# One core, eight batches: the filter loaded in four parts, and a new hand-kept order of the work

## The chip, the cores and the metric

The kernel runs on 1 core of one Trainium2 chip, as one launch. The time is device microseconds (us) of that core, the median over runs. The kernel before was run three times: 953.13, 957.69 and 958.69 us, median 957.69 us.

## What is computed

For each of 8 batches with S = 3136 rows, D = 256 features and 64 features of z:

```python
scores = z @ z.T / S                     # 3136 x 3136, symmetric
attn   = maximum(scores, 0) ** 2
x      = u * (attn @ v)
proj   = x @ w_proj                      # 256 -> 768, cut into x1, x2, x3
conv   = irfft(rfft(x2, axis=1) * rfft(filter_fft, axis=0), n=S)
out    = (x1 * conv * x3) @ w_out
```

All inputs and the output are float32; the kernel multiplies in bf16 and sums in float32. The filter is one matrix of 3136 x 256, the same for all batches, and its spectrum H is worked out once, beside batch 0.

## The kernel before

**Tiles.** The 3136 queries of a batch are cut into seven chunks (`CHUNKS`, 512 wide but for the last two, 256 and 320). For each chunk TensorE (PE) makes scores, two key tiles of 128 at a time, into one of three PSUM pairs `ps_s` (`score_mm`, L1632). ACT or DVE takes the positive part into `R_t` (L1790, L1792), ACT or DVE squares it into `A_t` (L1799, L1801). PE then multiplies `A_t` by v into the accumulator `ps_o_t` (`weigh`, through the helper at L462). Since the scores are symmetric, a chunk's squares are also the squares of later chunks, turned. SP sends them through a transposing DMA (`mirror`, L1739) into the mirror tiles M1 (for the next chunk) and M2e or M2o (for the one after), which the trace calls `M_t`, `M2e_t` and `M2o_t`; `weigh` reads them in place of new scores. M1, M2e and M2o have one buffer each, `A_t` has nine. An `A_t` buffer is free when its weighing is done and its transposes have landed.

**From chunk to output.** When a chunk is weighed, DVE multiplies it by u (`xe`, L1843) into `xT_t`. PE projects it to the gates and to x2 (`add_proj`); x2 goes through the first stage of the Fourier transform (`dft1`, matrix T1), and SP puts the result to DRAM (L950). When all seven chunks of a batch are there, `add_spectrum` loads the columns (L979; L994 in the last batch), runs the second stage forward, multiplies by H, runs it back, and puts the result (L1300). `add_end` loads that by chunk (L1014), runs the last stage (matrix T4), multiplies by the gates (L1351), multiplies by `w_out` and stores (L1383). Batch b's spectrum and end run beside batch b+1's attention; only the last batch has nothing beside it but work held back for it: the ends of three chunks of batch 6 (kind Z) and the gates of batch 7 (kind G).

**What sets the order.** A planner in the kernel's Python (`Plan`) gives out the work. The string `ORDER` says, letter by letter, what kind of work PE does next (S scores, W and v the two halves of a weighing, A, B, Q, Z, G and their second halves a). The string `ENGINES` says for each eviction whether ACT or DVE does it. SP, POOL, ACT and DVE take what is ready first by the planner's own reckoning of durations and DMA landings (`LATE_...`, `moves`, `late`). So the instruction streams of all engines are fixed when the kernel is built; on the chip each engine goes through its stream in order and waits where data is missing. What the planner takes for a landing changes only the order.

**POOL's casts.** Float32 input comes in as bf16 through casting DMAs that POOL issues: v (`load_rows`, L561), u (`cast_u`, L542), z (`cast_rows`, L542), the filter (`load_filter`, L635). They are issued in bundles: when the u product of a chunk is made, POOL copies one element of it (`await_x`, L551, "the tick" below) and then issues that chunk's bundle. In batch 0 the ticks of chunks 0, 1 and 2 also carry a part of the filter each (`filt_cuts`), and the third part carries `w_out` with it. The bundle that a chunk's tick carries for the next batch's v is set by `cuts`.

**The last batch's end.** `FINAL` is the order in which the chunks of batch 7 are ended: 0, 2, 4, 6, 1, 3, 5.

**Fillers.** Where the planner sees PE idle, it puts in matmuls of the identity (L662), whose results nobody reads.

Of the kernel before, what the change touches and what calls it, by code (L numbers as in the profile page):

```python
# [24 lines left out]
LATE_PUT, LATE_LOAD, LATE_TURN, LATE_M, LATE_C, LATE_D2 = 1.2, 1.2, 1.3, 0.3, 0.8, 1.0  # L25
# [9 lines left out]
FINAL = (0, 2, 4, 6, 1, 3, 5)  # L35
# [7 lines left out]
    "ASSASSSWWvSAWAWSvSvSvWSWWSvSWvSvWSvWWSvSWvWSvvSSSWSvWWWWWAWavSvAWWSWBvWSvSavWvWSSvvvvvBBaAaaWSWWAWSavWWWAAav"  # L43
    "aSWWSWSvvAvavSWSvAWWavSvSvvvBSSWABWavSWWWBSSvavvvBSWWWWaWSWSvvWvvSvASWaSvBvaSWvSWAWWWWWaBWaSvWvWWSvAvvSSavWv"
    "BvaSWvASaSAAaavvSSAaWWWWWWSSvvvWWAASvvaWvWaAvvvQSaWWWSWWWAAavWavWvQWSQvvWSSvWWSvAWavvSvvSvAaSSSWWWSvWvAWvSvW"
    "aSWWWSSvAvavAvWSSWWaWQSvQvvSvQASaWWWSWSSvWAWaWvSvWWSvSSvWSvAvWAWaSvWavSvvvQQAaWSWSvWSAWaWQSvWQWWWSQvSvvvWWQv"
    "QWWvSQvvvvASAaaWWQQvWvSWWSQvWvSWSvWQQvvWvSWQWQWWSvvQvSvAAaaWWQWWSQvAvavSWWSvSvWSvSAvaSWWWWASvSWavSWSvSAvavAB"
    "aaAWWavvWASWaASWaAvvWaBWvaWBWSavvSvSWSBvBaaAWavSBWaWWASvaWASWvWvSWavSWWWSBWSavvWASvavvvvABSaaWWAWaASvaSWAvaA"
    "WAaaWSvWSvWSvvSAvSaWSWWBSvvWaBWvSavvSSBaSWWWWSWSSvWvvvWSSWBvWWWSSvaWWSBvvaAvaSvSvvAQAaWaWWSWSAWWSavWQvSvvvvS"
    "SSWWWWSWWQvSvAvvvvAaSaWWWQWQvvWQSSWvvWWWQQvWvWSSvSvWWvSQvQvvAAaSaWWWQQWWWSQvSvvSWQWvvWAWavSAvWWWvSvSavvSvAAa"  # L50
    "AaWaSWWWWWAWSavSvWQvSvWvvSWQSvvvSAAaSWavWWAWaSvvWWSSSWvWWASvvvSaWWWvWSSvvvAvBSaaWWSWSWWWBSvavSvWSvSWAvaAvSWa"
    "BWSvaAvaAWWaWSBvavAvvaAAaSaWSWWSvBAaaSWvWSSvWSWWASvaWvAvavBSWWavSBvaWWvSSvvABaaWBWWSaSvvWSWBSaWAvaSvvQQvWWWS"
    "WQAvaSvWvABaWaWQvSvQvAASaaWWWSSvWWSvAvaAvQWWQvSWWQvvWvQBaWaWSvWBSvaSvvAAaSaWWQSSvWWSvQQvvWQWWSWQvSvWvAWWSvaA"
    "vSvaQWWSvQvAASaaWWWWSvvSWvSBvWWWSavSvvSWABvSaWaAvaAAaWSavWWSSvWWSWvSSvWBvaWWWSWAWAaWvavvSASavvvvSABaaWWSSvvW"
# [294 lines left out]
def kernel(  # L349
# [16 lines left out]
    NT = (N2 + 1) // 2  # L366
# [259 lines left out]

    def load_filter(t0, t1):
        x = rows_n1(moe_filter_fft)
        n = min(8, NT - 1 - t0)
        for j in range(2):  # L630
            a = NT + t0 if j else NT - t0 - n
            src = x[:, a : a + n]
# [495 lines left out]


    gates = {}  # L1130
    inverses, stores_late, last_load = [], [], []

    def add_proj(b, c, xt, x_):
        cw, nt = CHUNKS[c], len(tiles[c])
# [782 lines left out]
```

## Time and profile before

| What | Value |
|---|---|
| runs | 953.13, 957.69, 958.69 us |
| the profiled execution's own time | 959.67 us |
| its span, first to last instruction | 957.9 us |
| PE busy | 920.8 us, 11974 matmuls |
| DVE, ACT, POOL busy | 836.7, 825.9, 202.6 us |
| bytes moved by DMA | 168.40 MB, of these 37.30 MB by POOL's queue |

The profiled execution is 1.98 us over the median of the three runs, and 1.8 us of its time lie outside the span. The views used below are: the page (busy times, and the span in 40 slices); the windows (busy time of each engine in a stretch, with the granted clock of PE and the mean busy share of the 16 DMA engines); the waits (who waited for whom); the chain that ended last, in order of time; the timeline of one engine (start, duration, what; in brackets the idle time before it and what ended that); and the DMA view of a stretch. SPq and POOL rows that say DMA are the issue of a DMA, not its transfer.

### The profile page before, as it was taken

The numbers are of one execution on the slowest core, as the hardware profiler recorded it, in microseconds if no ns is written. First come the engines' busy times: TensorE is split into PE (matmuls) and PEld (weight loads), VectorE is DVE, ScalarE is ACT, GpSimd is POOL, SyncE is SP. The second block draws the span as 40 slices with busy tenths as digits, with TensorE's granted clock in tenths as the row PEclk, the third lists the DMA queues.
The fourth block names the chain that finished last, engine by engine and source line by source line (L and its number), as shares of the span: only waits on it lengthen the run. The fifth ranks groups of instructions, "written<-read, shape, count | busy, mean of one in ns | idle before, by whom it ended". The sixth has DMA issues, their size and how long they took to land.

```text
span 957.9 us, 28971 instructions
## 1 busy us (share of the span) xinstructions
PE 920.8 (96%) x11974; PEld 543.9 (57%) x11974; DVE 836.7 (87%) x1182; ACT 825.9 (86%) x927; POOL 202.6 (21%) x438
## 2 busy tenths in 40 slices
PE   7995999999999999999999999999999999999986
PEld 3442654557655675557655576546755566556644
DVE  8994699997999999999999779999889888899684
ACT  6783689999899898898989989999899999999672
POOL 5231211212122121222021120212212221001130
PEclk8997999999999999999999999999999999999997
DMA  9899778999999599998899997999899968887767
GB/s 156 144 173 119 158 131 147 178 199 170 183 190 182 116 187 180 210 200 167 162 190 201 202 207 171 186 169 187 185 165 183 185 123 174 181 205 146 208 187 225
DMA packets 321701, 168.40 MB, mean 176 GB/s; under 512 B 231990, under 2 KB 297334, under 8 KB 321568
## 3 DMA queue, kind: packets, MB, share of 16 engines
q1 hardware_dynamic: 290656, 127.54, 65.2%
q0 software_dynamic: 29872, 37.30, 26.3%
q8 instruction: 94, 1.54, 0.7%
q10 hardware_dynamic: 1040, 1.70, 0.6%
q14 instruction: 39, 0.32, 0.1%
HBM read 90.26 MB, written 53.35 MB: 150 GB/s over the span
## 4 chain that ended last, share of the span: by engine, by line
PE 82%; DMA 6%; DVE 5%; ACT 2%; issue 2%; SPq 2%; ACTq 0%; DVEq 0%; POOL 0%; POOLq 0%
PE ps_o_t L462 49%; PE ps_s L462 20%; PE ps_s L1632 10%; PE ps_s L1033 3%; DMA M2e_t<-A_t 2%; DMA spec<-gs_t 1%; DVE R_t L1792 1%; DVE xT_t L1843 1%; DMA zT_t<-zn_t 1%; DMA A_t<-spec 1%; SPq L1439 1%; DVE A_t L1801 1%; ACT R_t L1790 1%; DMA M_t<-A_t 0%; DMA spec<-uT_t 0%
## 5 line engine op out<-in xcount | busy, mean ns | idle before, releaser
L462 PE MATMUL ps_o_t<-A_t,v_t 64*128 64x512 bf16 (+4 forms) x4736 | 506.4, 355 | 0.6 <-DVE xT_t L1843 0.4
L462 PEld LDWEIGHTS <-v_t 64*128 64x128 bf16 (+1 forms) x6510 | 295.2, 98 | 217.7 <-issue 20.0
L1790 ACT ACTIVATE R_t<-ps_s 128x1024 f32<-128x1024 f32 (+4 forms) x353 | 331.8, 962 | 41.5 <-PE ps_s L1632 34.9
L1799 ACT ACTIVATE A_t<-R_t 128x1024 bf16<-128x1024 f32 (+3 forms) x283 | 275.8, 994 | 28.1 <-DMA M2e_t<-A_t 11.4
L1801 DVE TENSOR_TENSOR A_t<-R_t 128x1024 bf16<-128x1024 f32 (+4 forms) x209 | 229.6, 1116 | 15.1 <-ACT R_t L1790 12.6
L1632 PE MATMUL ps_s<-zT_t 64*128 64x512 bf16 (+5 forms) x1209 | 191.2, 355 | 14.0 <-ACT R_t L1790 10.4
L1792 DVE TENSOR_SCALAR R_t<-ps_s 128x1024 f32<-128x1024 f32 (+4 forms) x159 | 175.5, 1113 | 33.0 <-PE ps_s L1632 27.9
L551 POOL COPY tick<-xT_t 1x1 bf16<-1x1 bf16 x54 | 9.5, 177 | 640.2 <-DVE xT_t L1843 640.2
L462 PE MATMUL ps_s<-xT_t,wp 64*128 64x512 bf16 (+2 forms) x848 | 118.7, 351 | 0.4 <-ACT R_t L1790 0.4
L1632 PEld LDWEIGHTS <-zT_t 64*128 64x128 bf16 (+1 forms) x1209 | 67.6, 97 | 51.2 <-issue 6.3
L502 ACT ACTIVATE x_t<-ps_s 128x1024 bf16<-128x1024 f32 (+3 forms) x82 | 76.5, 941 | 19.9 <-PE ps_s L462 18.7
L462 PE MATMUL ps_o_t<-M_t,v_t 64*128 64x512 bf16 (+4 forms) x864 | 93.3, 352 | 0.0
L1843 DVE SCALAR_TENSOR_TENSOR xT_t<-ps_o_t,uT_t 128x256 bf16<-128x256 f32 (+2 forms) x224 | 71.3, 380 | 11.3 <-PE ps_o_t L462 5.6
L1256 DVE TENSOR_TENSOR xh<-xh,H 128x2048 bf16<-128x2048 bf16 x60 | 72.3, 1217 | 1.8 <-ACT xh L502 1.6
L1165 DVE TENSOR_TENSOR gate_t<-ps_s,x_t 128x512 bf16<-128x512 f32 (+2 forms) x104 | 59.7, 615 | 14.6 <-PE ps_s L462 10.4
L1351 DVE TENSOR_TENSOR yT_t<-ps_s,gate_t 128x1024 bf16<-128x1024 f32 (+2 forms) x51 | 55.1, 1084 | 14.0 <-PE ps_s L462 12.0
L462 PE MATMUL ps_s<-wp,xT_t 64*128 64x256 bf16 x800 | 65.3, 269 | 0.4 <-DVE s_t L506 0.2
L462 PEld LDWEIGHTS <-wp 64*128 64x128 bf16 x896 | 47.3, 94 | 30.2 <-issue 3.2
L542 POOL DMA_DIRECT2D un_t<-in_u_dram x112 | 59.9, 554 | 9.5 <-issue 6.8
L561 POOL DMA_DIRECT2D v_t<-in_v_dram x112 | 58.7, 542 | 8.7 <-issue 7.0
L462 PE MATMUL ps_s<-wo,yT_t 64*128 64x256 bf16 x732 | 58.6, 270 | 0.7 <-DVE yT_t L1351 0.4
L462 PE MATMUL ps_o_t<-M2e_t,v_t 64*128 64x512 bf16 (+2 forms) x440 | 52.0, 353 | 1.5 <-DVE xT_t L1843 1.4
(174 smaller groups left out, 887.4 us busy)
## 6 DMA issues: line engine op xcount, KB each, us to landing
out_dram<-ost_t SPq DMA_DIRECT2D x56, 256.0 KB
spec_in_t<-spec SPq DMA_DIRECT2D x56, 192.0 KB
spec<-gs_t SPq DMA_DIRECT2D x56, 192.0 KB
v_t<-in_v_dram POOLq DMA_DIRECT2D x80, 128.0 KB, 5.0
un_t<-in_u_dram POOLq DMA_DIRECT2D x80, 128.0 KB, 5.7
spec<-s_t SPq DMA_DIRECT2D x40, 256.0 KB
conv_in_t<-spec SPq DMA_DIRECT2D x34, 256.0 KB
out_dram<-ost_t POOLq DMA_DIRECT2D x12, 256.0 KB, 3.7
```

The source lines that it names most:

```text
L462: last = matmul(o[ds(i, n)], w[:, ds(i, n)], m, **kw)
L502: nc.scalar.activation(out_, in_, AF.Copy)
L542: nc.gpsimd.dma_start(out=t[ds(j * N1, N1), lo - t0 : hi - t0, :], in_=x[:, n2 : n2 + hi - lo, :])
L561: nc.gpsimd.dma_start(out=t[ds(j * N1, N1), ds(v_at(a), (b - a) * D)], in_=r[:, n2 + a - lo : n2 + b - lo, :].rearrange("p t d -> p (t d)"),)
L1165: nc.vector.tensor_tensor(g[:, :, ::-1] if h == 0 else g, p, x, ALU.mult)
L1256: nc.vector.tensor_tensor(x, x[:, 1].unsqueeze(1).to_broadcast([P, 2, 2, 2 * D]), h, ALU.mult)
L1632: matmul(o[ds(m, n)], zt[h, ds(t * P + m, n)], q, start=True, stop=True)
L1790: nc.scalar.activation(r, p, AF.Relu)
L1792: nc.vector.tensor_single_scalar(r, p, 0.0, ALU.max)
L1799: nc.scalar.activation(a, r, AF.Square)
L1801: nc.vector.tensor_tensor(a, r, r, ALU.mult)
L1843: nc.vector.scalar_tensor_tensor(x[:, ::-1] if h == 0 else x, f, inv_s2, ut, ALU.mult, ALU.mult)
```

## The change

The diff does five things. The filter comes in four parts where it came in three: the old third part, rows 16 to 24 and `w_out`, becomes one of rows 16 to 20 on the tick of chunk 2, and one of rows 20 to 24 with `w_out` on the tick of chunk 3. Batch 1's v comes one or more chunks later. `FINAL` becomes 5, 6, 0, 2, 4, 1, 3, and the last batch's gates stand in their queue in that order. Four of the planner's guesses of landings are raised. `ORDER` and `ENGINES` are other strings of the same letters. The products stay the same; fewer of the matmuls of scores and weighings are cut into two of 64 columns (the planner does that where they stand beside work of kind Q), and there are 9 fillers where there were 16.

```diff
-LATE_PUT, LATE_LOAD, LATE_TURN, LATE_M, LATE_C, LATE_D2 = 1.2, 1.2, 1.3, 0.3, 0.8, 1.0
+LATE_PUT, LATE_LOAD, LATE_TURN, LATE_M, LATE_C, LATE_D2 = 2.2, 1.2, 1.3, 0.3, 0.8, 2.5
...
-FINAL = (0, 2, 4, 6, 1, 3, 5)
+FINAL = (5, 6, 0, 2, 4, 1, 3)
...
-    "ASSASSSWWvSAWAWSvSvSvWSWWSvSWvSvWSvWWSvSWvWSvvSSSWSvWWWWWAWavSvAWWSWBvWSvSavWvWSSvvvvvBBaAaaWSWWAWSavWWWAAav"
...
+    "ASSASWSSAWSvSASSWSWSvvWWWWSvSWBvWSvSvSWSvvvSWWvvSAWSvaASWWSWWavSvvWWSvSWWWSvWvWvWvSvvvSAaBSWWavWWSvBSvWWWWaW"
...
     def load_filter(t0, t1):
         x = rows_n1(moe_filter_fft)
-        n = min(8, NT - 1 - t0)
+        n = min(t1, NT - 1) - t0
...
-    filt_cuts = ((0, 8), (8, 16), (16, NT))
-    filt_ld = [Task(lambda e, x=x: load_filter(*x), {"POOL": 1.6}, moves=3.3, late=4.0) for x in filt_cuts]
+    filt_cuts = ((0, 8), (8, 16), (16, 20), (20, NT))
+    filt_ld = [Task(lambda e, x=x: load_filter(*x), {"POOL": 1.6}, moves=0.42 * (x[1] - x[0]), late=4.0) for x in filt_cuts]
...
-        return on("SP", go, 0.55, deps, [home.slots], moves=0.235 * nt, late=1.0 if home is cut_in else -1.0), box
+        return on("SP", go, 0.55, deps, [home.slots], moves=0.235 * nt, late=1.0 if home is cut_in else -0.4), box
...
-                [t1_done, filt_ld[min(t0 // 8, 2)]], (filt_hold[t0 // 8], 0) if t0 % 8 == 4 or nt == 1 else None,
+                [t1_done, filt_ld[min(t0 // 8, 2) + (t0 >= 20)]], (filt_hold[t0 // 8], 0) if t0 % 8 == 4 or nt == 1 else None,
...
+            if late:
+                late_gates.extend([(c, a), (c, a3)])
...
-            cuts = ((0, 0, 4, 8, 16, 22, NT, NT), (0, 4, 8, 12, 16, 20, NT, NT))[b > 0]
+            cuts = ((0, 0, 0, 4, 8, 16, NT, NT), (0, 4, 8, 12, 16, 20, NT, NT))[b > 0]
...
+                    late_gates.sort(key=lambda x: FINAL.index(x[0]))
+                    plan.queues["G"] = [t for _, t in late_gates]
...
-            if calls or b == 0 and c < 3:
+            if calls or b == 0 and c < len(filt_ld):
```

**SP, batch 0, chunk 2 and what follows it.** The rows from the mirrors of chunk 2 (into M1 954 and M2e 990) to those of chunk 3 (into M1 1189). `zT_t` is batch 1's z, `uT_t` a chunk's u, `spec1_0` and `specf` are the puts of a chunk and of the filter. Before:

```order
L1739 DMA_TRANSPOSE M1_t_954<-A_t_793 128x8x128
L1739 DMA_TRANSPOSE M1_t_954<-A_t_817 128x8x128
L1739 DMA_TRANSPOSE M2e_t_990<-A_t_923 128x8x128
L1503 DMA_TRANSPOSE zT_t_1009<-zn_t_807 128x4x128
L950 DMA spec1_0_59<-s1_t_983 128x4x256
L1439 DMA_TRANSPOSE uT_t_1044<-un_t_849 128x8x128
L1739 DMA_TRANSPOSE M2e_t_990<-A_t_934 128x8x128
L950 DMA specf_63<-s1_t_1137 128x4x256
L1739 DMA_TRANSPOSE M1_t_1189<-A_t_1075 128x8x128
L1739 DMA_TRANSPOSE M1_t_1189<-A_t_1087 128x8x128
```

and now (the changed kernel's line numbers are two higher in its later part; chunk 2's mirrors go into M2e 896 and M1 947, chunk 3's into M1 1164):

```order
L1741 DMA_TRANSPOSE M2e_t_896<-A_t_872 128x8x128
L950 DMA specf_63<-s1_t_844 128x4x256
L1741 DMA_TRANSPOSE M2e_t_896<-A_t_874 128x8x128
L1741 DMA_TRANSPOSE M1_t_947<-A_t_781 128x8x128
L1741 DMA_TRANSPOSE M1_t_947<-A_t_798 128x8x128
L1505 DMA_TRANSPOSE zT_t_997<-zn_t_817 128x4x128
L1441 DMA_TRANSPOSE uT_t_1016<-un_t_841 128x8x128
L950 DMA spec1_0_59<-s1_t_968 128x4x256
L950 DMA specf_63<-s1_t_1077 128x4x256
L1741 DMA_TRANSPOSE M1_t_1164<-A_t_991 128x8x128
L1741 DMA_TRANSPOSE M1_t_1164<-A_t_1108 128x8x128
```

Both M2e transposes of chunk 2 now stand ahead of its M1 transposes, and ahead of z, u and the chunk's put; before, the second one stood behind all of these. The first M1 transpose of chunk 3 follows two puts where it followed one.

**POOL, batch 0, the ticks of chunks 2 and 3.** `xh2` and `gate_t` hold the filter's last rows, `wo16` is `w_out`, `v16_t` batch 1's v. The bundle of chunk 2's tick before:

```order
L551 COPY tick_165<-xT_t_1056 1x1
L635 DMA xh2_120<-in_moe_filter_fft_dram 64x8x256
L635 DMA xh2_120<-in_moe_filter_fft_dram 64x2048
L639 MEMSET gate_t_174 64x256
L640 DMA gate_t_174<-in_moe_filter_fft_dram 64x256
L641 DMA wo16_205<-in_moe_w_out_dram 128x2x256
L561 DMA v16_t_828<-in_v_dram 64x1024 x2
L542 DMA un_t_1128<-in_u_dram 64x1024 x2
L542 DMA zn_t_1144<-in_z_dram 64x256 x2
L542 DMA zn_t_1144<-in_z_dram 64x512
```

and the bundles of chunks 2 and 3 now:

```order
L551 COPY tick_165<-xT_t_1025 1x1
L635 DMA xh2_120<-in_moe_filter_fft_dram 64x4x256
L635 DMA xh2_120<-in_moe_filter_fft_dram 64x1024
L561 DMA v16_t_1088<-in_v_dram 64x1024 x2
L542 DMA un_t_1099<-in_u_dram 64x1024 x2
L542 DMA zn_t_1130<-in_z_dram 64x256 x2
L542 DMA zn_t_1130<-in_z_dram 64x512
L551 COPY tick_165<-xT_t_1270 1x1
L635 DMA xh2_120<-in_moe_filter_fft_dram 64x4x256
L635 DMA xh2_120<-in_moe_filter_fft_dram 64x1024
L639 MEMSET gate_t_174 64x256
L640 DMA gate_t_174<-in_moe_filter_fft_dram 64x256
```

In bf16 bytes at the landing side the bundle of chunk 2's tick falls from 1.34 MB to 0.92 MB. `w_out` and half of the filter's last part move to the tick of chunk 3, whose bundle grows from 0.75 MB to 0.92 MB. The bundle of chunk 1 falls from 1.18 MB to 0.92 MB, since it carries no v any more.

**SP, the last batch's end.** `spec2_1` is the convolved batch 7 in DRAM, each `A_t` here one chunk of it. Before:

```order
L1014 DMA A_t_17973<-spec2_1_62 128x4x256
L1014 DMA A_t_17975<-spec2_1_62 128x4x256
L1014 DMA A_t_17987<-spec2_1_62 128x4x256
L1014 DMA A_t_17997<-spec2_1_62 128x3x256
L1014 DMA A_t_18016<-spec2_1_62 128x4x256
L1014 DMA A_t_18019<-spec2_1_62 128x4x256
L1014 DMA A_t_18034<-spec2_1_62 128x2x256
```

and now:

```order
L1014 DMA A_t_17870<-spec2_1_62 128x2x256
L1014 DMA A_t_17878<-spec2_1_62 128x3x256
L1014 DMA A_t_17898<-spec2_1_62 128x4x256
L1014 DMA A_t_17900<-spec2_1_62 128x4x256
L1014 DMA A_t_17910<-spec2_1_62 128x4x256
L1014 DMA A_t_17918<-spec2_1_62 128x4x256
L1014 DMA A_t_17926<-spec2_1_62 128x4x256
```

The two short chunks, two and three tiles of 64 KB, are loaded first now, and four tiles come last.

78 lines of the change are left out of this document (39 added, 39 removed).

## The prediction

> **What bounds the kernel now.** I read the page first, then the windows to find where PE stands, then waits, chain and timelines of that place.
>
> ```profile
> PE 920.8 (96%) x11974; PEld 543.9 (57%) x11974; DVE 836.7 (87%) x1182; ACT 825.9 (86%) x927; POOL 202.6 (21%) x438
> PE   7995999999999999999999999999999999999986
> ```
>
> PE is the bound: idle for 37.1 of 957.9 us. The work on it stays the same, so a new order can only win part of these 37 us, or of time in which PE's clock is low. The slice with the 5 is the one hole outside the ends. The windows (columns: PE, PEld, DVE, ACT, POOL busy, granted clock, DMA share, GB/s) give its size:
>
> ```profile
> 48.00:72.00 24.00, 23.49 (x227) 10.75 (x225) 21.92 (x43) 21.40 (x25) 8.17 (x16) 1.00 1.01 173
> 72.00:96.00 24.00, 12.88 (x105) 5.82 (x103) 10.37 (x14) 9.30 (x10) 4.33 (x10) 0.79 1.01 119
> 456.00:480.00 24.00, 24.00 (x312) 15.12 (x309) 22.58 (x31) 21.76 (x26) 2.24 (x6) 1.00 0.80 159
> 912.00:936.00 24.00, 18.97 (x333) 11.74 (x329) 19.82 (x21) 16.09 (x18) 8.57 (x17) 1.00 0.65 189
> 936.00:960.00 24.00, 13.87 (x193) 9.47 (x191) 9.61 (x14) 5.93 (x6) 1.05 (x2) 0.74 0.68 204
> ```
>
> From 72 to 96 us, in batch 0, PE is idle for 11.1 us, at a clock of 0.79 while it runs; the DMA engines are full from 48 on. The middle of the program is full on PE. The tail, from 912 on, has the rest. Waits and chain of the hole:
>
> ```profile
> PE ps_s L1632 <- ACT R_t L1790: 10.4, 2, 10.0
> ACT A_t L1799 <- DMA M2e_t<-A_t: 11.4, 1, 11.4
> 64.75 17.04 DMA M2e_t<-A_t
> 82.83 1.01 ACT R_t L1790
> 83.89 0.58 PE ps_s L1632
> ```
>
> One mirror transpose is on its way for 17.04 us. Until it lands, its source cannot be overwritten, so ACT, whose next instruction squares into that one of nine `A_t` buffers, stands for 11.4 us; the eviction queued behind it on ACT comes late, no PSUM pair gets free, and PE stands for 10.0 us. Why the transpose is late stands in SP's and POOL's timelines:
>
> ```profile
> 60.12 1.19 SPq L1503 DMA_TRANSPOSE zT_t<-zn_t  x1
> 61.41 0.52 SPq L950 DMA_DIRECT2D spec<-s_t  x1
> 62.05 2.65 SPq L1439 DMA_TRANSPOSE uT_t<-un_t  x1
> 64.75 1.65 SPq L1739 DMA_TRANSPOSE M2e_t<-A_t  x1
> 70.92 10.84 SPq L1739 DMA_TRANSPOSE M_t<-A_t  x2
> 63.69 1.23 POOL L635 DMA_DIRECT2D xh<-in_moe_filter_fft_dram  x2 [0.29 <-issue]
> q1 hardware_dynamic: 5529, 1.69, 63.1%
> q0 software_dynamic: 1520, 1.34, 56.5%
> ```
>
> (The last two rows are the DMA queues from 62 to 84 us: packets, MB, share of 16 engines.) SP is busy issuing z, a put and u up to the late transpose, which leaves at 64.75, about one us after POOL has begun to cast the filter's third part. POOL's bundle is 1.34 MB, and the two queues' shares sum to over 100%. The following mirror transposes take 10.84 us to issue at all.
>
> **The change part by part**, against the profiled execution's 959.67 us.
>
> *The late transpose, −8.0 us.* SP now issues both M2e transposes of chunk 2 before z, the put and u. Those three took from 60.12 to 64.75, so the transpose leaves at least 4.6 us earlier, ahead of the casts. Even at 17.04 us on its way it would leave a hole of 10.0 − 4.6 = 5.4 us. The casts of that bundle fall by 0.42 MB. POOL's queue held 56.5% of 22 us for 1.34 MB, 9.3 us per MB, so 0.42 MB are 3.9 us of all 16 engines; with the 0.26 MB of v that chunk 1's bundle no longer carries, 6.3 us. Either takes most of the 5.4 us.
>
> Next late are chunk 3's mirrors, M1 1164, whose sources are squared after the tick. In the order, 103 matmuls' worth of 512 columns lie between the first weighing of the second source (A 1108) and the first use of that mirror; before there were 93 (A 1087). What a matmul takes is shown by the chain, at low clock and at full clock:
>
> ```profile
> 84.47 3.57 PE ps_o_t L462 x20
> 95.37 2.16 PE ps_o_t L462 x20
> ```
>
> At 2.16 / 20 = 0.108 us the 103 are 11.1 us. A transpose on its way for 17.04 − 3.9 to 17.04 − 6.3, that is 13.1 to 10.7 us, leaves PE waiting 0 to 2 us. I keep 2.0 of the 10.0 us. Bounds: nothing left (−10.0), or half left because these transposes meet the same crowd (−5.0).
>
> *The clock, −2.3 us.* After the hole 20 matmuls took 3.57 us instead of 2.16, and the window's 0.79 over 12.88 us of work is a loss of 2.7 us. A wait of 2 us or less should keep most of it; I take 2.3, bounds 0 and 2.7. The Trainium skill ("TensorE: Matmul & The Clock Gate", What's actually happening) has the clock at half for about 3.4 us after an idle window, an estimated loss of 1.7 us where the trace has 2.7, and with 1.7 the sum would be 0.6 us higher at most; the trace decides.
>
> *The fourth filter part, +0.3 us.* Its two casts (0.45 us after the tick, 1.23 us of issue) must land before PE transforms rows 20 to 24.
>
> ```profile
> xh<-in_moe_filter_fft_dram POOLq DMA_DIRECT2D x2, 256.0 KB, 6.7
> DMA to landing us min/median/max: 3.0/4.4/12.5
> 91.88 1.09 DVE xT_t L1843 x3
> ```
>
> (The first row is the filter's third part, the second the casts of u from 60 to 140 us, the third three of the four steps of a u product.) That is 8.4 us after the tick. From the end of chunk 3's weighing to that product lie 108 matmuls, 11.7 us; the u product takes about 1.4. So some 2 us are spare; only a landing of 12.5 us would cost 3.5, and PE's order is fixed, so all of PE would wait. I take 0.3, bounds 0 and 3.5.
>
> *Batch 1's v, +0.5 us.* The tick of chunk 5 now carries nine tiles of v, seven DMAs, where it carried three:
>
> ```profile
> 121.76 0.18 POOL L551 COPY tick<-xT_t 1x1 bf16<-1x1 bf16 x1 [3.34 <-DVE xT_t L1843]
> 122.21 1.03 POOL L561 DMA_DIRECT2D v_t<-in_v_dram  x2 [0.27 <-issue]
> DMA to landing us min/median/max: 3.3/4.3/4.9
> 134.22 1.47 PE L462 MATMUL ps_o_t<-A_t,v_t 64*128 64x512 bf16 x12
> ```
>
> Batch 1's first weighing, at 134.22, waits for all of them; it came 12.5 us after the tick, and the order keeps that distance (105 matmuls for 107). Seven issues of 0.52 us after 0.45 us, and a landing of 4.3, make 8.4 us; 0.39 MB more at 9.3 us per MB, were the engines full, 12.0. So it just fits; I take 0.5, bounds 0 and 2.5.
>
> *The end, −0.4 us.* PE waits twice for the loads of the convolved batch:
>
> ```profile
> 934.28 0.86 PE L462 MATMUL ps_o_t<-T,A_t 64*128 64x128 bf16 x16 [2.09 <-DMA A_t<-spec]
> 937.90 0.61 PE L462 MATMUL ps_s<-T,A_t 64*128 64x128 bf16 x8 [1.81 <-DMA A_t<-spec]
> 950.15 0.82 DVE L1351 TENSOR_TENSOR uT_t<-ps_s,gate_t 128x640 bf16<-128x640 f32 x1 [1.05 <-issue]
> 952.75 0.81 ACT L502 ACTIVATE R_t<-ps_s 128x768 f32<-128x768 f32 x1 [1.78 <-PE ps_s L462]
> 946.18 1.23 DVE L1351 TENSOR_TENSOR uT_t<-ps_s,gate_t 128x1024 bf16<-128x1024 f32 x1
> 949.95 1.02 ACT L502 ACTIVATE gs_t<-ps_s 128x1024 f32<-128x1024 f32 x1 [1.66 <-PE ps_s L462]
> ```
>
> The third load ended 3.62 us after the first two had let PE go. The first three are 576 KB now instead of 768 KB: 1.4 us less at 1.81 us for 256 KB. Against that, the chunk that ends last had 320 columns and has 512: 1.23 for 0.82 on DVE, 1.02 for 0.81 on ACT, four matmuls of 256 columns (0.2), and a store a third longer (0.2): +1.0. Bounds −1.4 (the end is hidden) and +1.0 (the loads are not faster). The fillers that go stood in these waits and cost nothing; the waits that they covered stay.
>
> *At nothing:* the start and the middle; PE is full there (24.00 of 24 us from 456 on), and DVE and ACT keep their sums.
>
> Sum: −8.0 − 2.3 + 0.3 + 0.5 − 0.4 = −9.9, so 949.8 us where the profiled execution took 959.67. The median of the runs lies 1.98 us lower, at 957.69: **947.8 us**.
>
> **The rivals.** *The jam moves and half of it stays.* The bytes are only shifted: chunk 3's transposes still follow a bundle of 0.92 MB, and chunk 4's meet one of 0.92 MB where they met 0.75. For it speaks that the DMA share was 1.01 in two windows on end, so the queue was behind before the third part came; against it, that 1.34 MB is the largest bundle of all and goes. With 5 us of hole left and the low clock kept, 959.67 − 5.0 + 0.4 = 955.1, on the median 953.1. The Trainium skill ("DMA: Bandwidth & Descriptors", Issuing engines are not separate DMA queues) says that DMAs of all issuing engines run on the same 16 engines and interleave; the shares of 63.1% and 56.5% agree, and by that alone moving casts in time helps only as far as the later stretch has room.
>
> *The hole is not the change's to take.* The runs spread from 953.13 to 959.67, 6.5 us, with one and the same order: if most of the hole is the luck of one execution, the order gains little. Against it: 10.0 + 2.7 us of hole are twice that spread, so even the fastest run should hold half. Only the v and filter terms and some 2 us of gain remain: 956.5.
>
> *Slower: the jam repeats one chunk later.* The fourth part's tick issues 0.92 MB just as chunk 4's mirrors go out (M1 1456, M2e 1395). If one is again on its way for 17 us, its `A_t` buffer is missing again: between A 1387's first weighing and its successor's lie 157 matmuls, 17.0 us, so it decides from about 17 us on. With a hole of 10.0 and 2.7 of clock there, and only the 4.6 us from SP's order won before: 957.7 + 12.7 − 4.6 = 965.8. Against it, and only partly, the DMA engines from 84 to 106 us, in 40 slices:
>
> ```profile
> DMA  9999008900000000008899699999954921408829
> ```
>
> They run dry from 88 to 94 us, so there is room; but PE's hole had held the work up, and without the hole they would be busier.
>
> **How the numbers follow.** Forecast 0.50, the jam half kept 0.31, not the change's to take 0.12, the jam repeated 0.07. The likeliest case by itself spans 943 to 951. The range of 940.5 to 957.0 is: below, all of hole and clock and 1.4 at the end, 957.7 − 14.1 = 943.6, less 3 for the spread of runs; above, the second rival. About 1% is what a measurement of this kernel can tell, here 948.1: faster gets 0.8 of the forecast and a quarter of the first rival, 0.48; slower the last rival, 0.07; within 1% the rest, 0.45.
>
> **What would show it.** Right: in batch 0 the wait of ACT for `M2e_t<-A_t` is gone or under 2 us, no PE wait over 3 us outside the ends, the clock 0.9 or more in 72 to 96, PE idle in all below 30 us. The v term shows as a wait of batch 1's first `ps_o_t` on `v_t`, the filter term as one of `ps_s<-xh,T`, the end in the two waits on `A_t<-spec` and the time after the last one. Wrong: a wait of ACT on another `M..<-A_t` of 5 us or more before 130 us, or windows in the middle under 23 us of PE.

## The result, and the profile after

The changed kernel takes 959.66 us (median of 20 runs, 953.53 to 968.34); the kernel before, run beside it 20 times, takes 954.42 us (943.96 to 964.28). The ratio is 1.0076, with a 95% interval of 1.0047 to 1.0104: slower, where 947.8 us and a gain were forecast. (Ratios leave out, for each kernel, runs more than 1.5% above its own lowest, which takes more from a kernel whose runs spread widely; the medians alone give 1.0055.)

The profiled execution of the changed kernel took 957.30 us. Its page, busy times and PE in 40 slices:

```profile
PE 923.1 (97%) x11846; PEld 545.1 (57%) x11846; DVE 839.8 (88%) x1187; ACT 827.0 (87%) x922; POOL 204.2 (21%) x440
PE   7999999999999999999999999999999999999985
```

The slice with the 5 is gone. SP's timeline of the place, and a row of POOL's:

```profile
53.78 1.29 SPq L1741 DMA_TRANSPOSE M2e_t<-A_t  x1
55.16 0.53 SPq L950 DMA_DIRECT2D specf<-s_t  x1
55.74 1.30 SPq L1741 DMA_TRANSPOSE M2e_t<-A_t  x1
57.14 2.60 SPq L1741 DMA_TRANSPOSE M_t<-A_t  x2
59.91 1.19 SPq L1505 DMA_TRANSPOSE zT_t<-zn_t  x1
61.20 1.26 SPq L1441 DMA_TRANSPOSE uT_t<-un_t  x1
...
63.94 1.18 POOL L635 DMA_DIRECT2D xh<-in_moe_filter_fft_dram  x2 [0.29 <-issue]
```

Both M2e transposes leave ahead of z and u, the second one 9.0 us before the 64.75 at which the late one left, and long before the casts of the filter's third part at 63.94. By the landings that the traces record for each DMA, the second one is now on its way for 3.2 us, where the late one took 17.04. So the change did at this place what it says. The windows (columns as in the prediction) of the place and of the middle of the program:

```profile
72.00:96.00 24.00, 23.66 (x228) 10.76 (x224) 15.77 (x22) 19.87 (x22) 6.49 (x14) 1.00 0.93 158
144.00:888.00 744.00, 736.32 (x9700) 444.51 (x9696) 669.21 (x922) 678.87 (x755) 142.60 (x308) 1.00 0.94 177
```

The kernel before, the same stretch of the middle:

```profile
144.00:888.00 744.00, 740.27 (x9902) 446.16 (x9898) 677.96 (x928) 686.21 (x768) 146.09 (x316) 1.00 0.95 178
```

From 72 to 96 us PE goes from 12.88 to 23.66 us at full clock. But from 144 to 888 us it is busy for 4.0 us less. The gain at the start is there, and something behind it takes it back.

### The profile page after: what moved, and what is told of

Same layout as the page of the kernel before. It is cut to its first block, busy times and chain, and to the rows that moved or that the text cites. A ratio compares the mean times of both kernels' runs of the same rounds, so it can differ in the third digit from the quotient of the medians.

```text
span 955.5 us, 28714 instructions
## 1 busy us (share of the span) xinstructions
PE 923.1 (97%) x11846; PEld 545.1 (57%) x11846; DVE 839.8 (88%) x1187; ACT 827.0 (87%) x922; POOL 204.2 (21%) x440
## 4 chain that ended last, share of the span: by engine, by line
PE 39%; DMA 6%; ACT 4%; DVE 2%; issue 1%; SPq 1%; DVEq 0%; ACTq 0%
PE ps_o_t L462 23%; PE ps_s L462 9%; PE ps_s L1634 5%; PE ps_s L1033 2%; ACT R_t L1792 1%; DMA spec<-s_t 1%; DMA spec_in_t<-spec 1%; DMA uT_t<-un_t 1%; DMA M2o_t<-A_t 1%; DMA A_t<-spec 1%; ACT A_t L1801 1%; ACT xh L502 1%; SPq L1014 0%; DVE R_t L1794 0%; ACT gs_t L502 0%
## 5 line engine op out<-in xcount | busy, mean ns | idle before, releaser
L462 PE MATMUL ps_o_t<-A_t,v_t 64*128 64x512 bf16 (+3 forms) x4676 | 503.8, 355 | 2.4 <-DVE xT_t L1845 1.3
L1792 ACT ACTIVATE R_t<-ps_s 128x1024 f32<-128x1024 f32 (+4 forms) x355 | 336.0, 969 | 44.4 <-PE ps_s L1634 35.2
L1801 ACT ACTIVATE A_t<-R_t 128x1024 bf16<-128x1024 f32 (+4 forms) x278 | 273.7, 1004 | 18.4 <-DVE R_t L1794 12.7
L1803 DVE TENSOR_TENSOR A_t<-R_t 128x1024 bf16<-128x1024 f32 (+4 forms) x214 | 233.8, 1110 | 20.9 <-ACT R_t L1792 11.6
L1634 PE MATMUL ps_s<-zT_t 64*128 64x512 bf16 (+4 forms) x1204 | 193.9, 353 | 6.9 <-DVE R_t L1794 2.5
L462 PE MATMUL ps_s<-xT_t,wp 64*128 64x512 bf16 (+2 forms) x888 | 123.9, 350 | 2.6 <-DVE xT_t L1845 1.3
L462 PE MATMUL ps_o_t<-M_t,v_t 64*128 64x512 bf16 (+3 forms) x832 | 96.4, 354 | 0.0
L502 ACT ACTIVATE x_t<-ps_s 128x1024 bf16<-128x1024 f32 (+3 forms) x74 | 69.1, 941 | 22.7 <-PE ps_s L462 16.3
L1165 DVE TENSOR_TENSOR gate_t<-ps_s,x_t 128x512 bf16<-128x512 f32 (+2 forms) x112 | 64.5, 617 | 8.9 <-PE ps_s L462 8.4
L542 POOL DMA_DIRECT2D un_t<-in_u_dram x112 | 60.1, 557 | 6.2 <-issue 3.9
L502 ACT ACTIVATE xh<-ps_s 128x1024 bf16<-128x1024 f32 (+2 forms) x51 | 52.3, 1038 | 6.9 <-PE ps_s L1033 3.9
```

Of the source, the lines that this page charges most:

```text
L462: last = matmul(o[ds(i, n)], w[:, ds(i, n)], m, **kw)
L502: nc.scalar.activation(out_, in_, AF.Copy)
L542: nc.gpsimd.dma_start(out=t[ds(j * N1, N1), lo - t0 : hi - t0, :], in_=x[:, n2 : n2 + hi - lo, :])
L1165: nc.vector.tensor_tensor(g[:, :, ::-1] if h == 0 else g, p, x, ALU.mult)
L1634: matmul(o[ds(m, n)], zt[h, ds(t * P + m, n)], q, start=True, stop=True)
L1792: nc.scalar.activation(r, p, AF.Relu)
```

## The experiments

Most kernels below are compared by one measure, worked out for every batch: the time at which the u product of a chunk starts in DVE's timeline, less the matmuls that stand ahead of it in PE's order, counted at the full rate of 512 columns in 0.107 us for a matmul on half the array and half of that for one on a quarter; fillers count as work. Its growth over a batch is what that batch lost to waits, switches and low clock. "Batch 0" contains the start; "tail" is the time from the last u product to the end.

### Both kernels again

Nothing is edited.

> The kernel before, unchanged, profiled once more. Theory A (the 10 us hole of chunk 3 of batch 0 is one execution's luck): in this profile the wait of ACT for M2e in batch 0 is under 5 us or gone, and the time is 945 to 955 us. Theory B (the hole is in every execution): the wait is 8 to 12 us again and the time 955 to 960. Ratio to the kernel before 1.00 in both.

> The changed kernel, unchanged, profiled once more. Theory A (the new head is sound, the rest of the new order loses some 10 us in small holes after batch 1): chunks 0 to 6 of batch 0 lose under 22 us again, batches 2 to 7 lose 35 us or more where the kernel before loses 30, ratio 1.005 to 1.01. Theory B (the loss after batch 1 was one execution's): batches 2 to 7 lose 30 us, and the loss shows up in another place.

The kernel before took 955.26 us (949.97 to 964.13, ratio 1.0019 [0.9978, 1.0059]), the changed one 961.19 us (953.08 to 967.26, ratio 1.0055 [1.0018, 1.0092]), the kernel before beside both 956.54. The loss repeats. The profiled execution of the kernel before was 949.97 us this time. Its windows:

```profile
72.00:96.00 24.00, 20.56 (x186) 10.65 (x184) 14.68 (x20) 13.66 (x15) 6.14 (x13) 0.93 0.99 167
144.00:888.00 744.00, 740.52 (x9928) 448.71 (x9924) 675.87 (x925) 685.42 (x769) 146.90 (x317) 1.00 0.95 179
```

its waits from 60 to 100 us:

```profile
ACT A_t L1799 <- DMA M2e_t<-A_t: 3.8, 1, 3.8
PE ps_s L1632 <- ACT R_t L1790: 2.3, 1, 2.3
```

and the window of the changed kernel's, which took 966.71 us:

```profile
144.00:888.00 744.00, 731.09 (x9564) 436.32 (x9560) 663.25 (x910) 672.81 (x746) 140.17 (x303) 0.99 0.95 176
```

Two things are read from them. The hole of batch 0 is in the kernel before both times, at the same place and through the same wait, but its size is a draw: PE waited 10.0 us in the execution that the prediction used, 2.3 us in this one. (Four profiles further on have the old head and nine buffers too; there PE waits 3.0 to 10.3 us at this place.) And the middle is the same in both executions of the kernel before (740.27 and 740.52 us of PE), less in both of the changed one (736.32 and 731.09).

### Head and rest

The change can be cut at the 564th letter of `ORDER`, in batch 1, where both orders have used up the same letters. The head has the filter's parts, batch 1's v and the new order of batch 0; the rest has the new order of the later batches and `FINAL`. `head_new` is the kernel before with the new head, `head_old` the changed kernel with the old head:

```diff
-ORDER = ORDER_OLD
+ORDER = ORDER_NEW[:564] + ORDER_OLD[564:]
...
-    filt_cuts = ((0, 8), (8, 16), (16, NT))
+    filt_cuts = ((0, 8), (8, 16), (16, 20), (20, NT))
...
-            cuts = ((0, 0, 4, 8, 16, 22, NT, NT), (0, 4, 8, 12, 16, 20, NT, NT))[b > 0]
+            cuts = ((0, 0, 0, 4, 8, 16, NT, NT), (0, 4, 8, 12, 16, 20, NT, NT))[b > 0]
```

> The changed kernel's batch 0 (filter in four parts, v later, new order and landings up to letter 564 of 2693, which is chunk 6 of batch 1) and the old order from there to the end. Theory A (the new head wins, the later part loses): faster than the kernel before by 3 to 10 us, ratio 0.990 to 0.997. Theory B (the new head itself costs): slower by 3 to 6 us, ratio 1.003 to 1.007. Theory C (all is luck of landings): ratio 1.000 within its interval.

> The converse: the old batch 0 (filter in three parts, old order up to letter 564) and the new order, FINAL and gates from there. Theory A: slower than the kernel before by 8 to 12 us, ratio 1.008 to 1.013, since it has the old hole and the new losses. Theory B: ratio 0.998 to 1.002. Theory C: 1.000 to 1.005.

`head_new` took 954.91 us (950.91 to 960.09; ratio 1.001 [0.9979, 1.004]), `head_old` 973.01 us (ratio 1.0215 [1.0158, 1.0273]); the kernel before beside them 956.54. In these two the planner plans the other engines' streams anew behind the cut, so the rest was not quite either parent's; by the measure above, batches 1 to 7 of `head_new` lost 47.0 us, where the kernel before loses some 35. To have it exactly, the streams of both kernels were written out as lists and played back, head from one list and rest from the other:

```diff
-ORDER = (
+SEQ = (
...
     def go(self):
+        todo = [(by[int(n)], names[e]) for n, e in zip(nos, es)]
...
+        for t, e in todo:
...
+            self.run(t, e, s)
```

> The streams of two kernels joined exactly: up to letter 564 of 2693 (chunk 6 of batch 1) every engine's stream of the changed kernel, from there to the end that of the kernel before, instruction by instruction, so that no stream is planned anew (in head_new the planner's later decisions could shift). Theory A (parts add up: the new head wins 6 us, the new rest loses 10): 949 us where before has 955, ratio 0.990 to 0.997. Theory D (what the head wins is given back by later waits, whatever the order of the rest): ratio 0.999 to 1.002, and the batches after 1 lose 6 us more than in the kernel before.

> The converse joined exactly: the old streams up to letter 564, the new ones from there. Theory A: 965 us, ratio 1.008 to 1.013. Theory D: 960 us, ratio 1.003 to 1.007, as the changed kernel. If the 1.0215 of head_old was the join's doing, this one is well below it.

`x_head_new` (new head, old rest) took 953.26 us (948.63 to 956.38; 0.999 [0.9959, 1.0021]), `x_head_old` (old head, new rest) 964.45 us (952.46 to 970.48; 1.0066 [1.0024, 1.0108]), the kernel before beside them 956.36. So the loss is in the rest and comes with either head; the new head takes 3 us off the median (the ratio does not show it) and halves the spread of the runs (standard deviation 2.3 us, where the kernel before had 5.1 in the same session). One theory on record was that later waits give back what the head wins, whatever the order of the rest: a ratio of 0.999 to 1.002, and 6 us more lost behind batch 1. The ratio of `x_head_new` lies there, but its batches 1 to 7 lose 37.6 us, 2 to 3 more than before, and those of `x_head_old` 47.5; so the loss goes with the order of the rest. The re-planning in `head_old` cost another 8.5 us by the medians of two sessions, a miss of that way of cutting.

### Do the stores crowd the transposes?

Both kernels' streams without the output's stores of batches 0 to 5:

```diff
                 r = rows_n1(out[b])
+                if b < 6:
+                    return
```

> The streams of the kernel before, without the stores of the output of batches 0 to 5 (so six eighths of the output are left out and some 19 MB of writes with them); all else in the same order. Theory E (the later holes come from mirror transposes that are late because the DMA engines are crowded): faster by 3 to 8 us, ratio 0.992 to 0.997, and the batches after 0 lose under 33 us. Theory F (they come from the order of ACT's and DVE's own work): ratio 0.999 to 1.001.

> The same edit on the changed kernel. Theory E: it gains more than the kernel before does, 10 us or more, and comes out level with nostore_before or up to 6 us below it, since the head's gain is left; the holes of over 2 us after batch 0 are gone. Theory F: it stays 4 to 6 us above nostore_before.

950.24 us (942.11 to 957.41; ratio 0.9947 [0.9908, 0.9987]) and 954.47 us (951.34 to 957.00; 1.0011 [0.998, 1.0043]). Both gain by some 5 to 7 us, but with a DMA share of 0.84 in the middle instead of 0.94 or 0.95 the difference of the medians is still 4.2 us. The kernel before without stores, then the changed one:

```profile
144.00:888.00 744.00, 740.64 (x9915) 446.80 (x9912) 679.46 (x928) 687.24 (x769) 142.83 (x310) 1.00 0.84 153
144.00:888.00 744.00, 736.58 (x9725) 443.98 (x9721) 671.18 (x924) 681.02 (x758) 140.18 (x305) 1.00 0.84 152
```

PE's middle stays at 740.64 and 736.58. Crowding by the stores is not the cause of the difference.

### Where in the rest

The exact splice again, with the new order up to a later letter and the old one from there on.

> The streams of the changed kernel on all five engines up to the 1543rd letter of PE's order (the start of batch 5), then those of the kernel before, with its order of the convolved batch at the end. Spliced at letter 564 the same construction took 953.3, against about 960 for the whole changed kernel. Theory, the new order loses a little in every batch after the first, at places where an A_t buffer waits for its mirror transpose: about half of the 6.5 us, so 0.3% to 0.4% over the splice at 564, ratio to before 1.002 to 1.004. Rival 1, the loss sits in batches 5 to 7 or in the tail: ratio 0.999 as the splice at 564. Rival 2, it sits in batches 2 to 4: ratio 1.006.

> The changed kernel's streams up to letter 1782 (batch 5, chunk 6), then those of the kernel before. The profiles of the changed order show two recurring holes here: after batch 5's chunk 4 (an M2o transpose 9.5 to 10.0 us on its way, DVE waiting 3.7 to 4.4 us) and after batch 6's chunk 2 (10.0 to 12.0 us, ACT waiting 1.6 to 5.4). Theory, these two carry the loss and this splice holds the first only: 3 to 6 us over the splice at 1543, so 953 to 956. Rival 1, the loss comes later: 950. Rival 2, it all comes in batch 5: 960.

> The changed kernel's streams up to letter 2023 (batch 6, chunk 3), then those of the kernel before: both recurring holes are in it. Theory, they carry the loss: 958 to 962, as the splice at 2543. Rival, the loss comes in the last batch and a half: 950 to 953.

> The streams of the changed kernel up to letter 2543, the end of the last batch's chunks, then the tail of the kernel before, with its order of the convolved batch. Theory, the loss is spread over batches 2 to 7 and the tail is neutral: ratio to before 1.006 to 1.008, as the whole changed kernel. Rival, the tail's new order of the convolved batch is what costs: 0.999 to 1.001.

> The splice at letter 2543 once more, unchanged. If its 961.8 is the program's own: 959 to 964, ratio 1.007 to 1.014. If it was the measurement: 953 to 957, level with the splice at 2023. Its profile shows whether the loss stands in the same batches as the first time (batch 4: 12.9, batch 3: 9.0, batch 5: 9.0 us between PE's counted work and the clock) or in others.

| new order up to | median us (range) | ratio [95%] | batch 0 | batches 1 to 7 | tail |
|---|---|---|---|---|---|
| none (before; again) | 954.42; 955.26 | 1 | 32.8; 25.1 | 35.3; 34.5 | 60.1; 59.0 |
| 564, batch 1 | 953.26 (948.63 to 956.38) | 0.999 [0.9959, 1.0021] | 23.0 | 37.6 | 62.0 |
| 1543, batch 5 | 950.00 (946.93 to 955.70) | 0.9992 [0.9958, 1.0026] | 23.6 | 39.7 | 56.9 |
| 1782, batch 5's end | 955.79 (952.10 to 964.49) | 1.002 [0.9984, 1.0055] | 22.0 | 43.1 | 58.7 |
| 2023, batch 6 | 953.65 (951.47 to 959.30) | 0.9986 [0.9954, 1.0018] | 22.9 | 44.9 | 57.0 |
| 2543, batch 7's end | 961.81 (958.43 to 967.16) | 1.0119 [1.0069, 1.0168] | 25.1 | 50.8 | 59.8 |
| 2543, once more | 956.66 (952.97 to 966.09) | 1.0023 [0.9985, 1.0060] | 23.5 | 47.6 | 57.8 |
| all (after; again) | 959.66; 961.19 | 1.0076; 1.0055 | 21.0; 22.8 | 45.6; 53.3 | 59.3; 59.2 |

The last three columns are microseconds lost in the one profiled execution. In these profiles batches 1 to 7 lose more with each further piece of the new order up to letter 2543, and no piece carries it alone; since two profiles of the changed kernel differ by 7.7 us here, the single steps are not to be read. The windows of the spliced kernels show the same trend without any counting. Up to 1543:

```profile
144.00:888.00 744.00, 738.96 (x9847) 444.52 (x9845) 672.65 (x924) 685.14 (x765) 143.58 (x312) 1.00 0.96 178
```

up to 2023:

```profile
144.00:888.00 744.00, 735.03 (x9784) 442.28 (x9780) 670.61 (x923) 679.22 (x756) 142.25 (x308) 1.00 0.93 177
```

up to 2543, once more:

```profile
144.00:888.00 744.00, 734.78 (x9662) 442.41 (x9658) 668.12 (x915) 678.41 (x753) 142.67 (x309) 1.00 0.94 177
```

The medians do not follow step by step, and the repeat says why: the very same program gave 961.81 in one session (6 runs) and 956.66 in another, on another chip (12 runs), with intervals of the ratio that do not meet. By this, a single comparison here is good to some 0.5%, not to the width of its interval; whether chip, session or the few runs made the difference is open. That the changed kernel is slower rests on two sessions and on `x_head_old`, not on one ratio. "Half of the loss by 1543" was a miss in the medians (950.0, nothing lost), and "it comes after 2023", which the medians then seemed to say, fell with the repeat. The expectations for 1782 and 2023 counted on one and on both of the places shown below. Their splices hold none and one: SP's order of the first place is still the old one in the splice at 1782 (its 955.79 lies in the 953 to 956 that was expected, but not for that reason), that of the second in the splice at 2023 (953.65, where 958 to 962 was expected). The tail, with the new `FINAL`, is neutral throughout.

### What the places are

SP's timeline at batch 6, chunk 2. Before:

```profile
718.81 1.24 SPq L1739 DMA_TRANSPOSE M2o_t<-A_t  x1
720.15 1.24 SPq L1439 DMA_TRANSPOSE uT_t<-un_t  x1
721.49 3.06 SPq L979 DMA_DIRECT2D spec_in_t<-spec  x6
```

The changed kernel's repeat:

```profile
716.86 1.24 SPq L1441 DMA_TRANSPOSE uT_t<-un_t  x1
718.57 2.85 SPq L979 DMA_DIRECT2D spec_in_t<-spec  x6
721.53 1.26 SPq L1741 DMA_TRANSPOSE M2o_t<-A_t  x1
```

with this piece of its chain (start, duration, what),

```profile
721.53 11.99 DMA M2o_t<-A_t
```

and these waits:

```profile
ACT A_t L1801 <- DMA M2o_t<-A_t: 5.4, 1, 5.4
PE ps_s L1033 <- ACT xh L502: 4.3, 1, 4.3
```

The new order lets the M2o transpose leave behind six loads of the spectrum, where it left ahead of them. It is then on its way for 11.99 us, ACT stands for 5.4 us before the `A_t` buffer that it still reads, and PE for 4.3 us behind ACT. It is batch 0's hole at another place. The Trainium skill ("DMA: Bandwidth & Descriptors", Queues, rings and completion order) says that each DMA engine takes descriptors in the order of the ring and that the final signal lands only after every earlier write of that engine. The traces agree: ahead of the loads, in the kernel before, the same transpose was on its way for 2.75 us, and behind the six, which were issued within 2.85 us just before it, for 11.99 us.

Batch 5, chunk 4 has another. Before, M2o goes first:

```profile
640.22 1.25 SPq L1739 DMA_TRANSPOSE M2o_t<-A_t  x1
...
646.31 1.28 SPq L1439 DMA_TRANSPOSE uT_t<-un_t  x1
647.68 1.54 SPq L1300 DMA_DIRECT2D spec<-gs_t  x3
```

In the changed kernel it goes behind u, a transpose into M1, the stores of the spectrum and the put:

```profile
636.81 1.24 SPq L1441 DMA_TRANSPOSE uT_t<-un_t  x1
...
640.47 1.53 SPq L1302 DMA_DIRECT2D spec<-gs_t  x3
642.10 0.38 SPq L950 DMA_DIRECT2D spec<-s_t  x1
642.53 3.58 SPq L1741 DMA_TRANSPOSE M2o_t<-A_t  x1
```

Its chain, the wait, and the row of PE's timeline where the wait arrives:

```profile
642.53 9.52 DMA M2o_t<-A_t
```

```profile
DVE A_t L1803 <- DMA M2o_t<-A_t: 3.7, 1, 3.7
```

```profile
655.42 0.40 PE L1634 MATMUL ps_s<-zT_t 64*128 64x256 bf16 x2 [1.39 <-DVE R_t L1794]
```

To see whether the later place comes with the stretch that holds it, letters 2023 to 2543 alone were put into the kernel before:

> The kernel before, with only the stretch of its streams from letter 2023 to letter 2543 (batch 6, chunk 3, to the end of batch 7) taken from the changed kernel; filter, head, middle and tail are those of before. Theory, this stretch carries the loss by itself: 961 to 965, ratio 1.006 to 1.010, and its time shows in batches 6 and 7 of the profile, as a mirror that holds an A_t buffer. Rival 1, the loss is a matter of several small holes over batches 3 to 6, as the profiles have it, and the 962 of the splice at 2543 came from their adding up: within 0.3% of before. Rival 2, the stretch costs only behind the changed batches, whose work it hands on late: also within 0.3%; the profile of the repeated splice would then show its loss in batches 6 and 7.

It took 956.88 us (945.78 to 962.45; ratio 1.0026 [0.998, 1.0073]), so the time by itself does not show it. The profile, of an execution that took 962.22 us and has a large hole in batch 0 too, does show the wait in that stretch (SP's timeline, the waits, and the window of the middle):

```profile
722.55 3.08 SPq L1072 DMA_DIRECT2D spec_in_t<-spec  x6
725.73 1.27 SPq L1832 DMA_TRANSPOSE M2o_t<-A_t  x1
```

```profile
ACT A_t L1892 <- DMA M2o_t<-A_t: 3.4, 1, 3.4
PE ps_s L1126 <- ACT xh L595: 2.4, 1, 2.4
```

```profile
144.00:888.00 744.00, 736.62 (x9707) 442.99 (x9705) 672.71 (x919) 681.37 (x761) 144.95 (x314) 1.00 0.96 177
```

The splice at 2023, which has the new order up to here and the old one from here on, has the transpose ahead of the loads again, and no wait for it:

```profile
719.58 1.26 SPq L1832 DMA_TRANSPOSE M2o_t<-A_t  x1
722.29 3.05 SPq L1072 DMA_DIRECT2D spec_in_t<-spec  x6
```

Over all twenty profiles, by the recorded landings: where this M2o stands ahead of the six loads, it is on its way for 2.75 to 2.81 us in all ten, and nobody waits for it; behind them, for 6.0 to 12.0 us in all ten. ACT waits for it (1.6 to 5.4 us, PE up to 4.3) in the six with nine `A_t` buffers in which it took 8.5 us or more, not in the two with nine in which it took 6.0 and 7.4; in the one with eight it waits 2.9 us after 8.8, in the one with ten not at all after 10.3. At the place in batch 5 it is 2.7 to 4.6 us ahead of the stores (ten profiles) and 5.7 to 10.0 behind them (ten), and DVE or ACT waits in six of the latter (0.6 to 4.4 us); in the changed kernel's repeat it took 7.9 us and nobody waited. SP's order of these two alone was not swapped; that the place in the queue makes the time rests on these twenty profiles and on the stretch, where other instructions moved too.

### How it reaches PE: the buffers

One `A_t` buffer less, streams kept:

```diff
-    A_p = Pool("A", 9, [P, 1024], BF16)
+    A_p = Pool("A", 8, [P, 1024], BF16)
```

> The kernel before with its five streams kept instruction by instruction, and eight A_t buffers instead of nine. Theory, PE's holes come where ACT or DVE waits for an A_t buffer that a late mirror transpose still reads: each transpose then has one weighing less of time before its buffer is wanted, about an eighth, so the holes in all batches grow and new ones appear: 8 us or more above the kernel before (over 0.8%), and in 144 to 890 us the waits of ACT and DVE on mirrors rise from 3.4 us to over 10. Rival, these waits go with holes that have another cause (evictions, the PSUM pairs, SP's queue): within 0.3% of the kernel before.

> The changed kernel's streams with eight A_t buffers instead of nine. Theory, as for the kernel before with eight, and since the changed order already has the smaller slack in batches 2 to 7, it rises by more: 10 us or more above the changed kernel, ratio to before 1.018 or above. Rival 1, other cause: ratio 1.005 to 1.010, as with nine. Rival 2, the buffers matter but the two orders have the same slack: it rises by just as much as the kernel before does.

984.65 us (ratio 1.0353 [1.0297, 1.0409]) and 982.99 us (1.0337 [1.0285, 1.039]). Three of the waits of the kernel before with eight, over the whole program:

```profile
ACT A_t L1892 <- DMA M_t<-A_t: 17.7, 8, 4.3
DVE A_t L1894 <- DMA M_t<-A_t: 9.6, 7, 2.6
DVE A_t L1894 <- DMA M2e_t<-A_t: 8.8, 2, 6.2
```

One buffer less costs the kernel before 31 us and the changed one 22 to 23, and from 144 to 890 us the waits of ACT and DVE on mirrors rise from 3.4 to 27.0 us in the kernel before: a late transpose does reach PE through the `A_t` buffer that it holds. The two orders come out level with eight; the theory had the changed one rise by more, and it rises by less. One more buffer, paid for with the second buffer of the puts' staging:

```diff
-    A_p = Pool("A", 9, [P, 1024], BF16)
+    A_p = Pool("A", 10, [P, 1024], BF16)
...
-    s1_p = Pool("s1", 2, [P, 4, D], BF16)
+    s1_p = Pool("s1", 1, [P, 4, D], BF16)
```

> The kernel before with its streams kept, ten A_t buffers instead of nine, and one s_t buffer (the staging of the puts) instead of two, which pays for the tenth. Eight buffers cost 3.5%. Theory, a late mirror reaches PE through the buffer that it holds, and nine are still too few at some places: the hole of batch 0's chunk 3 (5.7 to 15.0 us in the profiles) shrinks below 4 us and the smaller ones go: 4 to 10 us faster than before, ratio 0.990 to 0.996. Rival 1, nine are enough except for one place: 0.997 to 1.000. Rival 2, the single s_t buffer makes evictions wait for the puts before it, and takes back more than the tenth A_t brings: ratio over 1.003, with ACT or DVE waiting for DMA spec<-s_t.

> The changed kernel's streams with ten A_t buffers and one s_t buffer. Theory, its loss in batches 5 to 7 passes through held A_t buffers: it falls by 8 us or more from its 960 and comes out level with the kernel before with ten buffers, within 0.3%. Rival 1, the loss has another way to PE: it stays 0.6% or more above A10_before. Rival 2, the single s_t buffer costs, as there.

971.29 us (ratio 1.0181 [1.0132, 1.023]) and 968.13 us (1.0147 [1.0096, 1.0198]): a failure as a test of ten buffers. The kernel before with ten:

```profile
DVE s_t L599 <- DMA specf<-s_t: 9.6, 3, 5.5
ACT s_t L595 <- DMA spec_in_t<-spec: 6.4, 1, 6.4
```

The single staging buffer makes the evictions into it wait for DMAs, and batch 0 alone loses 39.4 us by the measure above; what ten `A_t` buffers are worth stays open.

## Why the prediction was wrong

**The step that failed is "At nothing: the start and the middle".** The prediction took the middle as safe, since PE was full there before, of which it showed one window of 24 us. That says nothing about the new order, which moves SP's instructions in all eight batches. Batches 1 to 7 lost 35.3 and 34.5 us before, 45.6 and 53.3 us in the changed kernel: on the mean of two profiles each, 14.6 us more. Two of the places are shown above; in the two profiles they make 6.5 us (4.4 and 2.1) and 7.3 us of what these batches lost. Three more chunks lose in both profiles of the changed kernel and hardly in those of the kernel before: chunk 6 of batch 3 (1.9 and 0.9 us, 0.1 before), chunk 5 of batch 4 (2.3 and 1.6, 0.3 before) and chunk 6 of batch 6 (1.7 and 2.9, 0.2 before). Other losses change from run to run (one of 4.6 us in batch 4 of the repeat).

Taken apart by PE's steps from one matmul to the next in the same four profiles, the 14.6 us are of three kinds. Waits over 0.15 us grow from 5.7 and 4.4 to 10.3 and 15.1 us. Half clock, of which the kernel before has none in batches 1 to 7, takes 1.7 us in the one profile (3.4 us at half, once) and 5.1 in the other (three times). The third kind is no wait: the steps between matmuls on different shapes of the array, 70 in the kernel before and 78 now, take 15.2 and 15.1 us beyond the counted work before, 17.5 and 17.9 now. So on the mean some 7.6 us are waits, 3.4 clock and 2.6 the eight further changes of shape, and 1.0 is left. What makes each of the waits outside the two places shown is not settled.

The start was not at nothing either: the chunks of batch 0 other than chunk 3, where the hole stood, lost 19.5 and 19.4 us before and lose 20.7 and 22.5 now, 2.2 more on the mean.

**The late transpose, −8.0, and the clock, −2.3.** Right in mechanism: hole, wait and low clock are gone in every profile with the new head. The prediction gave chunk 3's transposes into M1 still 10.7 to 13.1 us and kept 2.0 us of the hole for them; they take 2.7 to 2.8 us in the changed kernel, and the M2e transpose in its new place 2.8 to 3.5 us in all twelve profiles with the new head, and nothing of the hole is left. Its size, though, was taken from one execution, and a large one: by the measure, chunk 3 of batch 0 lost 13.3 us in it and 5.7 in the other, 0.3 in both of the changed kernel. Over the six profiles with the old head and nine buffers it lost 5.7 to 14.7 us, 10.2 on the mean; that the 10.3 put down for hole and clock come close to this is luck. Batch 0 as a whole lost 32.8 and 25.1 us before, 21.0 and 22.8 in the changed kernel: 7.1 us less on the mean, since its other chunks take back 2.2. The clock's part was too large in the execution that was used. Finer windows of the kernel before, right after its hole:

```profile
84.00:86.00 2.00, 2.00 (x11) 0.77 (x10) 1.25 (x2) 1.69 (x2) 0.00 (x0) 0.50 2.03 277
86.00:88.00 2.00, 2.00 (x16) 0.96 (x14) 0.67 (x1) 0.63 (x1) 0.00 (x0) 0.70 0.37 77
```

Half clock for 2 us and 0.70 in the next two (1.00 after that) make 1.6 us lost, not the 2.7 that the mean clock of the 24 us window gave. The estimate from the Trainium skill ("TensorE: Matmul & The Clock Gate", What's actually happening) was 1.7 us, and the trace agrees.

**The fourth filter part, +0.3, and batch 1's v, +0.5.** Nothing of either. (The upper bound of the first, 3.5, comes to 3.9 by the numbers that it is worked out from.) From 80 to 130 us the longest wait of PE in the changed kernel was for the u product, none for `xh` or `v_t`:

```profile
PE ps_o_t L462 <- DVE xT_t L1845: 0.9, 1, 0.9
```

**The end, −0.4.** Right: 60.1 and 59.0 us of tail before, 59.3 and 59.2 now, 0.3 less on the mean. The two waits on the loads fell from 3.9 us to

```profile
PE ps_s L462 <- DMA A_t<-spec: 1.8, 2, 1.2
```

and from 2.9 to 1.7 in the repeats, so by 1.7 us on the mean for the 1.4 put down; since the tail is only 0.3 shorter, some 1.4 came back, for the 1.0 worked out for the larger last chunk.

**The sum** by these measures is −7.1 + 14.6 − 0.3 = +7.2 us, beside +5.2 and +4.7 us in the medians of two sessions. (It is the difference of the profiled executions, 962.0 and 954.8 us on the mean, taken apart, and no second measurement.)

**The rivals.** "The hole is not the change's to take" was half right: the runs of the kernel before spread over 20 us, not the 6.5 of the three shown, and 959.67 was among the long ones; but the hole was the change's to take, all of it. "The jam repeats one chunk later" had the right kind of loss at the wrong place: not at the fourth filter part, where no mirror was waited for, but where M2o got behind other transfers in batches 5 and 6. Of the signs named in advance, those for batch 0 came out right (no wait for M2e, clock 1.00), but PE was idle for 32.4 us in all, not under 30, and a sign for being wrong showed: a window of the middle under 23 us of PE. The changed kernel has two such windows in its first profile and four in its second, the kernel before none and one, so the sign by itself does not tell the two apart. One window of the changed kernel's first profile, and the one of the kernel before's second:

```profile
648.00:672.00 24.00, 21.93 (x294) 16.58 (x292) 15.50 (x25) 16.02 (x21) 2.69 (x7) 0.93 0.68 143
744.00:768.00 24.00, 22.42 (x275) 12.81 (x273) 20.88 (x35) 21.10 (x24) 5.66 (x13) 1.00 0.85 140
```

No kernel here is shown to beat both. The new head with the old rest has the lowest medians (953.26 and, spliced at 1543, 950.00, 3.1 and 3.6 us under the kernel before beside them), but their ratios hold 1 in the interval.

## What to carry to other kernels

Where a change brings a new order of everything, the place that it cures is only one of its terms: go through each queue for the same ailment elsewhere (here, each mirror transpose that now stands behind a bundle of loads), also where the engine was full before. A hole that one profile shows is a draw from a spread; take its size from several executions, or from the spread of the runs, before you put it into a sum. And before believing a difference of half a per cent, measure the same program twice.

## What the runs showed of the hardware

A transposing DMA of 128 x 1024 in bf16 is on its way for some 2.8 us where nothing large stands ahead of it on its queue (M2o in batch 6, ten profiles, 2.75 to 2.81), for 5.7 to 12.0 us behind a bundle of loads or stores (M2o in batches 5 and 6, ten profiles each), and for 10.0 to 17.3 us in the first hole (the old head, eight profiles); so most of its time is its place in the queue. A change of PE between matmuls on a half and on a quarter of the array costs some 0.22 us beyond the counted work (15.2 us over 70 in the kernel before, 17.5 over 78 in the changed one). The same program's median moved by 5 us between two sessions on two chips (961.81 with 6 runs and 956.66 with 12), and the 95% intervals of the two ratios do not meet. The kernel before spread over 17 to 25 us in every session, with a standard deviation of 4.6 to 5.5; with the new head and the old rest (`head_new`, `x_head_new`) it is 2.7 and 2.3, so most of the spread goes with the old head. That it is the draw of its hole fits the 5.7 to 14.7 us that the profiles show there, but no run shows it alone.
